# Four raw buffers for w_out, and three Newton steps for the reciprocal root, in a fused attention and two-layer kernel

## The chip, the cores and the metric

The kernel runs on one core of a Trainium2 chip. TensorE (PE) does the matmuls, VectorE (DVE) and ScalarE (ACT) the elementwise work, GpSimd (POOL) some of the elementwise products, and SyncE (SP) issues the transfers. The metric is device time in microseconds (us); lower is better.

## The reference

```python
x = attention(q, k, v)            # 4 batches, 8 heads, 576 positions of 64; laid out as [2304, 512]
# layer 1 (512 -> 2048 -> 512); w_in and w_out come as 64-bit floats
h = x @ w_in
g = np.maximum(h, 0.0) + alpha * np.minimum(h, 0.0)
x = g @ w_out
# layer 2 (512 -> 1536 -> 512)
rms = np.sqrt(np.mean(x * x, axis=-1, keepdims=True) + 1e-06)
xn = x / rms * rms_g
g = xn @ w_gate
silu = g * (1.0 / (1.0 + np.exp(-g)))
return silu * (xn @ w_val) @ w_out2
```

The attention is a sum of two: one over positions averaged by fours, and a local one in which each position sees its three neighbours on either side.

## The kernel before

The 2304 tokens are six blocks of 384, each block two chunks of 192. Every dense product is made of three float16 matmuls (high by high, high by low, low by high), so every operand is split into a high and a low half: ACT writes the high half (L345) and DVE the low one (L346).

The first layer begins in `m1_first`. Its stages `h0`, `h1` and `h2` multiply three chunks by w_in (PE L1250, `hps`); ACT and DVE apply the slope and split the result into `g` tiles (L1254, L1256, L345, L346). A `g` tile holds four of the 16 blocks f of 128 hidden columns, and the tiles stay in memory until `o0` and `o1` multiply them by w_out (PE L1263, `acc`). For chunk 0 the four tiles lie in the weight pool under the tags u12 (f = 0 to 3), u0 (4 to 7), u1 (8 to 11) and u2 (12 to 15).

Before that the weights have to be prepared. They arrive as 64-bit floats and pass through a raw tile `wr`: SP loads half a piece (L999 for w_in, L1009 for w_out), ACT rescales its upper words (L1018), and two DVE instructions put together a 32-bit float (L1020, L1021). Then ACT sums the squares (L1031). w_in comes in six pieces whose decoded floats `wc` lie under u0 to u5, three blocks f in each: u1 holds f = 3, 4, 5 and u2 holds f = 6, 7, 8, until `split_in` has made the float16 halves `wi` of those blocks. w_out comes in pieces 0 to 4 of three blocks and piece 5 of one; half of a large piece is 768 columns of 8 bytes in 128 partitions (768 KB), loaded by two transfers of 512 KB and 256 KB. Its raw tiles have two homes in a pool with one buffer per tag: `xh` for the first halves and `x1` for the second (piece 5 uses `xh` for both). A half can be loaded only when DVE has read the half that was there before. When all 16 blocks are squared, `scale_out` (PE L319 `allps`, then short DVE instructions to L1082) gives the scales, and `split_out` turns each block into `wo` (L345, L346). The floats of block f lie one place behind the halves of block f, so one split has to read before the next can write.

In program order, the 30 preparation steps of w_out are woven into stage `h0`, `scale_out` and nine splits into `h1`, and the rest into `h2`. What runs when is settled by `issue_order`: it lists every instruction with its operands, takes the use of a buffer by two tiles in turn as a dependency, simulates the engines with its own costs, and fixes the order of every engine's queue (SP's too), best of 20 rounds. Each queue then runs strictly in that order. A tile that is given a buffer whose earlier tile still has later readers in program order is placed behind those readers.

The second layer's `rms_tasks` normalise a block: squares, a sum over partitions, then `ssum`, which finds one over the root in tile `ry` from a bit trick (L1200, L1202) and Newton steps of three DVE instructions each (L1205, L1206, L1207) on three columns. A matmul spreads it (L1213) and DVE applies it (L1224). There are six such blocks; the first belongs to stage `o1`.

Of the kernel before, what the change touches and what calls it, by code (L numbers as in the profile page):

```python
# [234 lines left out]
def kernel(  # L235
# [19 lines left out]
    NF = FF // 128  # L255
# [88 lines left out]
    def split(hi, lo, src, s):  # L344
        nc.scalar.activation(out=hi, in_=src, func=AF.Copy, scale=s)  # L345
        nc.vector.scalar_tensor_tensor(out=lo, in0=src, scalar=s, in1=hi, op0=ALU.mult, op1=ALU.subtract)  # L346
# [684 lines left out]
                nc.scalar.activation(out=o, in_=src, func=AF.Square, accum_out=acc[:, i:i + 1])  # L1031

    p1 = [Piece(w_in, f"u{i}", c0=i * UC, n=min(UC, FF - i * UC)) for i in range(6)]
    p1o = [Piece(w_out, None, f0=3 * i, nf=min(3, NF - 3 * i), raw=("xh", "x1" if i < 5 else "xh")) for i in range(6)]
    RING = (3, 4, 6, 7, 5, 12, 0, 1, 2, 8, 9, 10, 11)
    W2_ORDER = [0, 4, 8, 1, 5, 9, 2, 6, 10, 3, 7, 11]
    W2_AT = {i: n for n, i in enumerate(W2_ORDER)}
# [128 lines left out]
    def rms_tasks(m):  # L1166
        st = {}

        ne = KK if m == 0 else 1

        def sq(e):
            def f():
                a = x1_p.tile([128, BW], F32, tag=("ra", "rb")[e % 2 if ne > 1 else e > 0], name="ra")
                nc.scalar.activation(out=a, in_=x1_t[m][:, e], func=AF.Square)
                if ne == 1 and e == 0:
                    st["a"] = a
                    return
                if ne == 1:
                    nc.vector.tensor_tensor(out=st["a"], in0=st["a"], in1=a, op=ALU.add)
                    if e < KK - 1:  # L1180
                        return
                    a = st["a"]
                if "ps" not in st:
                    st["ps"] = ps_t.tile([128, NT, ne], F32, tag="at", name="ssps")
                for t in range(NT):
                    nc.tensor.matmul(st["ps"][:, t, e % ne:e % ne + 1], a[:, t * 128:(t + 1) * 128], ones,
                                     start=True, stop=True)
            return f

        NT = BW // 128  # L1190

        def ssum():
            v_ = x1_p.tile([128, 3, NT], F32, tag="ry", name="ry")
            x, y, t_ = v_[:, 0], v_[:, 1], v_[:, 2]
            p = st["ps"][:, :, 0]
            if ne > 1:
                nc.vector.tensor_reduce(out=x, in_=st["ps"], axis=AX.X, op=ALU.add)
                p = x
            nc.vector.tensor_scalar(out=x, in0=p, scalar1=1.0 / DM, scalar2=1e-6, op0=ALU.mult, op1=ALU.add)
            nc.vector.tensor_scalar(out=y.bitcast(I32), in0=x.bitcast(I32), scalar1=1, scalar2=None,  # L1200
                                    op0=ALU.logical_shift_right)
            nc.vector.tensor_scalar(out=y.bitcast(I32), in0=y.bitcast(I32), scalar1=-1.0, scalar2=float(0x5F3759DF),  # L1202
                                    op0=ALU.mult, op1=ALU.add)
            for _ in range(4):
                nc.vector.tensor_tensor(out=t_, in0=y, in1=y, op=ALU.mult)  # L1205
                nc.vector.scalar_tensor_tensor(out=t_, in0=t_, scalar=-0.5, in1=x, op0=ALU.mult, op1=ALU.mult)  # L1206
                nc.vector.scalar_tensor_tensor(out=y, in0=t_, scalar=1.5, in1=y, op0=ALU.add, op1=ALU.mult)  # L1207
            st["y"] = y

        def bcast():  # L1210
            ps = ps_t.tile([128, BW], F32, tag="at", name="rps")
            for t in range(NT):
                nc.tensor.matmul(ps[:, t * 128:(t + 1) * 128], st["y"][:, t:t + 1].to_broadcast([128, 128]), ident,  # L1213
                                 start=True, stop=True)
            st["r"] = ps

        def xn(e):
            def f():
                if e == 0:
                    p_ = (xt_p, "xt") if m >= NBLK - 2 else (x1_p, "xh")  # L1220
                    st["xh"] = p_[0].tile([128, 2, KK, BW], F16, tag=p_[1], name="xh")
                    xh_t[m] = st["xh"]
                x = x1_t[m][:, e]
                nc.vector.tensor_tensor(out=x, in0=x, in1=st["r"], op=ALU.mult)  # L1224
                split(st["xh"][:, 0, e], st["xh"][:, 1, e], x, 2.0 ** P_N)
            return f

        return [sq(e) for e in range(KK)] + [ssum, bcast] + [xn(e) for e in range(KK)]

    xh_t = {}  # L1230
# [343 lines left out]
```

## Time and profile before

| | |
|---|---|
| time, median of 3 runs | 1074.2 us (1073.49 to 1074.56) |
| the profiled execution | 1076.26 us, of which its span is 1074.6 us |
| PE busy | 990.3 us (92%) |
| DVE busy | 711.3 us (66%) |
| ACT busy | 476.9 us (44%) |
| POOL busy | 144.8 us (13%) |

A busy share is an average over stages. The rows below are times in us from the start of the span. A bracket in a row of an engine's timeline is idle time before the instruction and what ended it. The granted clock (PEclk) is a share of TensorE's full clock.

### The profile page before, as it was taken

To read this page: it belongs to the slowest core of one execution; us is meant where nothing else is said; L and a number is where in the kernel's file an instruction comes from. 1 tells how busy PE (TensorE), PEld (TensorE's weight loads), DVE (VectorE), ACT (ScalarE), POOL (GpSimd) and SP (SyncE) were. 2 spreads that over 40 slices of the span, in tenths; PEclk is the share of its full clock that TensorE was granted. 3 is DMA by queue.
4 is the path that set the end of the run, shared out by engine and by line. 5 is a ranking of instruction groups with operands and counts; after the bars stand their busy time and mean duration, and the time that the engine had idled before them with its cause. 6 is when DMAs were issued, how large, how long until landed. Compare 5 with 4: busy or idle time off the path is not lost.

```text
span 1074.6 us, 16316 instructions
## 1 busy us (share of the span) xinstructions
PE 990.3 (92%) x6232; PEld 617.2 (57%) x6232; DVE 711.3 (66%) x1533; ACT 476.9 (44%) x1178; POOL 144.8 (13%) x118
## 2 busy tenths in 40 slices
PE   2698999769999997989999999999999999999996
PEld 2465567556996554555655555565556655555553
DVE  1557899899988788999854699993344252352321
ACT  2975878324778855443455323341133331221211
POOL 2412221232000123212100232310000000000000
PEclk9999979689999998999999999999999999999998
DMA  9964454301464422312012212100010000100000
GB/s 166 191 145 131 131 166 149 113 30 59 122 185 142 143 88 74 118 45 91 14 50 58 95 34 74 30 1 1 1 30 1 1 1 1 31 1 2 28 1 30
DMA packets 49972, 74.54 MB, mean 69 GB/s; under 512 B 17682, under 2 KB 30886, under 8 KB 49894
## 3 DMA queue, kind: packets, MB, share of 16 engines
q1 hardware_dynamic: 49894, 73.50, 24.4%
q8 instruction: 49, 0.80, 0.3%
q14 instruction: 29, 0.24, 0.1%
HBM read 68.76 MB, written 4.72 MB: 68 GB/s over the span
## 4 chain that ended last, share of the span: by engine, by line
PE 73%; DVE 13%; DMA 7%; ACT 4%; issue 1%; SPq 1%; POOL 1%; ACTq 0%; POOLq 0%; DVEq 0%
PE gps L1342 21%; PE hps L1250 16%; PE acc L1263 15%; PE oacc L1367 10%; DMA out_dram<-ob 4%; DVE prod L508 2%; PE lsps L837 1%; PE avps L649 1%; PE sps L610 1%; DVE prod L495 1%; DMA wr<-in_moe_w_out_dram 1%; DVE wc L1021 1%; PE avps L808 1%; PE lops L891 1%; DVE ls L458 1%
## 5 line engine op out<-in xcount | busy, mean ns | idle before, releaser
L1250 PE MATMUL hps<-xt,wi 128*128 128x192 f16 (+1 forms) x1536 | 335.1, 298 | 8.5 <-DVE g L346 7.7
L1342 PE MATMUL gps<-xh,w 128*128 128x384 f16 x1728 | 338.7, 327 | 0.6 <-DVE uhl L1359 0.6
L1263 PE MATMUL acc<-ghl,wo 128*128 128x384 f16 (+1 forms) x960 | 239.7, 312 | 4.6 <-ACT ghl L345 2.4
L1342 PEld LDWEIGHTS <-w 128*128 128x128 f16 x1728 | 169.8, 99 | 117.6 <-issue 4.1
L1367 PE MATMUL oacc<-w,uhl 128*128 128x512 f16 x648 | 192.4, 379 | 4.0 <-ACT ob L1397 2.6
L1250 PEld LDWEIGHTS <-wi 128*128 128x128 f16 x1536 | 153.5, 103 | 72.8 <-issue 21.2
L1263 PEld LDWEIGHTS <-wo 128*128 128x128 f16 x1344 | 130.6, 100 | 75.1 <-issue 10.8
L1353 DVE SCALAR_TENSOR_TENSOR th<-th,gps 128x384 f32<-128x384 f32 x72 | 39.8, 552 | 146.5 <-ACT th L1351 146.5
L1351 ACT ACTIVATE th<-gps,tsc 128x384 f32<-128x384 f32 x72 | 41.9, 581 | 147.6 <-PE gps L1342 147.4
L1367 PEld LDWEIGHTS <-uhl 128*128 128x128 f16 x648 | 63.9, 99 | 71.8 <-issue 3.7
L1256 DVE SCALAR_TENSOR_TENSOR hps<-g,oma,hps 128x192 f32<-128x192 f32 (+1 forms) x128 | 66.1, 516 | 44.3 <-ACT g L1254 43.6
L1254 ACT ACTIVATE g<-hps 128x384 f32<-128x384 f32 x96 | 47.1, 490 | 106.1 <-PE hps L1250 105.4
L447 POOL TENSOR_TENSOR prod<-cq,ckv 128x896 f32<-128x896 f32 x24 | 54.2, 2259 | 288.4 <-ACT w L345 114.4
L1358 ACT ACTIVATE uhl<-gps 128x384 f16<-128x384 f32 x72 | 35.4, 491 | 108.1 <-DVE gps L1356 102.1
L1263 PE MATMUL acc<-g,wo 128*128 128x384 f16 (+1 forms) x384 | 67.1, 297 | 6.9 <-DVE wo L346 5.1
L495 POOL TENSOR_TENSOR prod<-ls,ckv 128x896 f32<-128x896 f32 x24 | 44.0, 1835 | 139.8 <-DVE lo L508 66.6
L508 DVE TENSOR_TENSOR prod<-prod 128x384 f32<-128x384 f32 (+1 forms) x108 | 58.4, 551 | 4.9 <-POOL prod L495 4.9
L1359 DVE TENSOR_TENSOR uhl<-gps,uhl 128x384 f16<-128x384 f32 x72 | 40.0, 555 | 31.5 <-ACT uhl L1358 31.5
L345 ACT ACTIVATE ghl<-hps,sc 128x384 f16<-128x384 f32 x72 | 41.7, 579 | 38.6 <-DVE hps L1256 37.6
L458 DVE TENSOR_REDUCE ls<-prod 128x14 f32<-128x896 f32 x54 | 57.3, 1075 | 0.0
L346 DVE SCALAR_TENSOR_TENSOR ghl<-hps,sc,ghl 128x384 f16<-128x384 f32 x72 | 43.9, 611 | 14.9 <-ACT ghl L345 14.5
L1020 DVE TENSOR_SCALAR wc<-wr 128x768 int32<-128x768 int32 (+1 forms) x38 | 21.2, 561 | 36.7 <-ACT wr L1018 36.6
(229 smaller groups left out, 1245.3 us busy)
## 6 DMA issues: line engine op xcount, KB each, us to landing
wr<-in_moe_w_out_dram SPq DMA_DIRECT2D x18, 512.0 KB
wr<-in_moe_w_in_dram SPq DMA_DIRECT2D x20, 384.0 KB
wr<-in_moe_w_gate_dram SPq DMA_DIRECT2D x8, 768.0 KB
wr<-in_moe_w_val_dram SPq DMA_DIRECT2D x8, 768.0 KB
ckv<-in_k_dram SPq DMA_DIRECT2D x7, 768.0 KB
ckv<-in_v_dram SPq DMA_DIRECT2D x7, 768.0 KB
wr<-in_moe_w_out_dram SPq DMA_DIRECT2D x20, 256.0 KB
out_dram<-ob SPq DMA_DIRECT2D x13, 256.0 KB
```

What stands on the lines that cost most here:

```text
L346: nc.vector.scalar_tensor_tensor(out=lo, in0=src, scalar=s, in1=hi, op0=ALU.mult, op1=ALU.subtract)
L447: engs[i].tensor_tensor(out=pr, in0=view(st["q"][:, j, t:t + TP], [[D, TP], [0, ND], [1, D]]), in1=view(st["k"][:, j, t:t + TP], [[D, TP], ...
L458: nc.vector.tensor_reduce(out=st["s"][:, j, t:t + TP], in_=st.pop(("p", i)), axis=AX.X, op=ALU.add)
L495: engs[i].tensor_tensor(out=pr, in0=view(st["s"][:, j, t:t + TP], [[ND, TP], [1, ND], [0, D]]), in1=view(st["v"][:, j, t:t + TP], [[D, TP] ...
L508: add = lambda o, a, c: nc.vector.tensor_tensor(out=o, in0=a, in1=c, op=ALU.add)
L1250: nc.tensor.matmul(ps[:, j], wi[:, f + j, a, kk * 128:(kk + 1) * 128], x[:, b_, kk, c0:c0 + n], start=(i == 0), stop=(i == 3 * KK - 1))
L1254: nc.scalar.activation(out=g, in_=ps, func=AF.Relu, scale=-1.0)
L1256: nc.vector.scalar_tensor_tensor(out=ps[:, j], in0=g[:, j], scalar=oma[:, f + j:f + j + 1], in1=ps[:, j], op0=ALU.mult, op1=ALU.add)
L1263: nc.tensor.matmul(acc[e], wo_f(f)[:, a, e * 128:(e + 1) * 128], hl[:, b_], start=(f == 0 and i == 0), stop=(f == NF - 1 and i == 2))
L1342: nc.tensor.matmul(ps, w2_t[i0 + f // 3].rearrange("p a (k c) -> p a k c", k=KK)[:, a, kk, (f % 3) * 128:(f % 3 + 1) * 128], xh[:, b_, kk] ...
L1351: nc.scalar.activation(out=th, in_=gp, func=AF.Tanh, scale=tsc[:, f // 3:f // 3 + 1])
L1367: nc.tensor.matmul(acc[tt], t[:, a, tt * 128:(tt + 1) * 128], w[:, b_, f % 3], start=(f in first and i == 0), stop=(f in last and i == 2))
```

## The change

Pieces 1 and 3 of w_out take their raw tiles from the tags u1 (first half) and u2 (second half); pieces 0, 2, 4 and 5 stay as they were. The loop of Newton steps runs three times.

```diff
-    p1o = [Piece(w_out, None, f0=3 * i, nf=min(3, NF - 3 * i), raw=("xh", "x1" if i < 5 else "xh")) for i in range(6)]
+    p1o = [Piece(w_out, None, f0=3 * i, nf=min(3, NF - 3 * i), raw=(("xh", "x1"), ("u1", "u2"))[i % 2] if i < 5 else ("xh", "xh")) for i in range(6)]
...
-            for _ in range(4):
+            for _ in range(3):
                 nc.vector.tensor_tensor(out=t_, in0=y, in1=y, op=ALU.mult)
                 nc.vector.scalar_tensor_tensor(out=t_, in0=t_, scalar=-0.5, in1=x, op0=ALU.mult, op1=ALU.mult)
                 nc.vector.scalar_tensor_tensor(out=y, in0=t_, scalar=1.5, in1=y, op0=ALU.add, op1=ALU.mult)
```

## Rows read from the trace of the kernel before

**Rows 1.** Stretches: busy time (instructions) of PE, PEld, DVE, ACT, POOL; PEclk; DMA share; GB/s.

```profile
100.00:130.00 30.00, 24.52 (x134) 15.54 (x134) 21.69 (x57) 23.65 (x87) 7.46 (x3) 1.00 0.48 137
130.00:190.00 60.00, 53.75 (x424) 39.68 (x423) 56.51 (x122) 46.51 (x133) 11.84 (x9) 0.89 0.48 153
190.00:210.00 20.00, 13.54 (x82) 11.12 (x82) 16.88 (x33) 6.25 (x13) 4.49 (x3) 0.61 0.36 118
210.00:270.00 60.00, 50.08 (x385) 35.49 (x384) 58.74 (x107) 21.54 (x37) 17.75 (x9) 0.90 0.16 54
300.00:400.00 100.00, 100.00 (x778) 69.37 (x776) 83.77 (x198) 75.03 (x196) 8.36 (x3) 1.00 0.43 139
500.00:1040.00 540.00, 534.14 (x3159) 309.19 (x3158) 296.85 (x611) 168.24 (x371) 41.73 (x23) 1.00 0.08 25
```

**Rows 2.** SP's timeline: issues of w_out's loads (start, duration, line, count).

```profile
105.65 0.38 SPq L1009 DMA_DIRECT2D wr<-in_moe_w_out_dram  x1
...
131.21 2.57 SPq L1009 DMA_DIRECT2D wr<-in_moe_w_out_dram  x4
142.38 4.71 SPq L1009 DMA_DIRECT2D wr<-in_moe_w_out_dram  x4
154.74 2.68 SPq L1009 DMA_DIRECT2D wr<-in_moe_w_out_dram  x4
165.01 0.82 SPq L1009 DMA_DIRECT2D wr<-in_moe_w_out_dram  x2
...
190.66 0.34 SPq L1009 DMA_DIRECT2D wr<-in_moe_w_out_dram  x1
```

**Rows 3.** SP's waits, 90 to 200 us: in total, times, longest.

```profile
SPq L1009 <- DVE wo L1021: 26.2, 8, 6.2
```

**Rows 4.** PE's timeline, 200 to 240 us.

```profile
201.84 0.61 PE L319 MATMUL allps<-s,ones 128*128 128x16 f32 x2 [2.78 <-ACT sqs L1031]
...
207.78 5.83 PE L1263 MATMUL acc<-g,wo 128*128 128x384 f16 x24 [1.31 <-ACT wo L345]
...
238.01 1.46 PE L1263 MATMUL acc<-g,wo 128*128 128x384 f16 x4 [3.79 <-DVE wo L346]
```

**Rows 5.** Waits of all engines, 100 to 300 us: in total, times, longest.

```profile
ACT wo L345 <- DVE wo L346: 18.6, 11, 4.1
PE acc L1263 <- DVE wo L346: 5.1, 3, 3.8
PE acc L1263 <- ACT wo L345: 1.9, 2, 1.3
```

**Rows 6.** The chain that ended last: a run of `acc` matmuls later on.

```profile
707.82 1.46 PE acc L1263 x9
```

**Rows 7.** DVE's timeline: splits of w_in and of `g`, decoding of w_out.

```profile
86.56 0.75 DVE L346 SCALAR_TENSOR_TENSOR wi<-wc,swi,wi 128x512 f16<-128x512 f32 x1
126.64 0.74 DVE L346 SCALAR_TENSOR_TENSOR wi<-wc,swi,wi 128x512 f16<-128x512 f32 x1
159.78 0.61 DVE L346 SCALAR_TENSOR_TENSOR g<-hps,sc,g 128x384 f16<-128x384 f32 x1
163.99 0.95 DVE L1021 SCALAR_TENSOR_TENSOR wo<-wr,wo 128x768 int32<-128x768 int32 x1
169.20 0.95 DVE L1021 SCALAR_TENSOR_TENSOR wo<-wr,wo 128x768 int32<-128x768 int32 x1
170.07 0.61 DVE L346 SCALAR_TENSOR_TENSOR g<-hps,sc,g 128x384 f16<-128x384 f32 x1
```

**Rows 8.** Tile `ry`: count, duration in ns (min/median/max), first and last start.

```profile
L1205 DVE TENSOR_TENSOR ry<-ry x24: 100/160/165, 283.8 to 943.4; 128x3 f32<-128x3 f32 x24
L1206 DVE SCALAR_TENSOR_TENSOR ry<-ry x24: 153/159/165, 284.0 to 943.5; 128x3 f32<-128x3 f32 x24
L1207 DVE SCALAR_TENSOR_TENSOR ry<-ry x24: 152/164/1329, 284.5 to 943.7; 128x3 f32<-128x3 f32 x24
```

## The prediction

> **What bounds the kernel now.** I read the page's engine totals and its 40 slices first: PE is busy 92% of the span, and nearly all that is missing lies before 500 us. So I cut the span into stretches [rows 1]. From 500 to 1040 us PE is busy 534.14 of 540 us and from 300 to 400 us all of 100: there PE alone sets the end, and no saving on DVE, ACT or a queue is worth anything. Between 100 and 270 us it is another picture. From 210 to 270 us DVE is busy 58.74 of 60 us and PE only 50.08; from 130 to 190 us DVE 56.51 and PE 53.75; and from 190 to 210 us PE is busy 13.54 of 20 us at a mean granted clock of 0.61, that is, for part of the time at the lower of its levels, 1.2 GHz. In that short stretch DVE too has 3.12 us free. So somebody else is late there.
>
> Third came the queue of transfers and its waits. The loads of w_out leave SP in groups [rows 2]: 131.21 for piece 1, 142.38 for piece 2, 154.74 for piece 3, 165.01 for the first half of piece 4, 190.66 for the last half piece. That is a step of (165.01 - 131.21) / 3 = 11.3 us per piece. SP waits 26.2 us in eight waits at those loads for the last DVE instruction of decoding [rows 3], which is what empties a raw buffer. So the pieces do not overlap: a load, a decode, the next load into the same buffer.
>
> Fourth came PE's own timeline at the end of that chain [rows 4]. PE stands 2.78 us before the sum of squares that opens `scale_out`, 1.31 us before the first matmul with w_out, and 3.79 us in the middle of that stage for a split of w_out. The list of waits adds them up [rows 5]: 5.1 us on DVE's half of the split and 1.9 us on ACT's. The splits are a chain of their own, because each must read a place before the next writes it: ACT waits 18.6 us for DVE there.
>
> **The change part by part.** *Raw buffers.* No work of an engine is removed: the same 22 loads, 12 rescalings and 24 DVE instructions of decoding. What changes is who waits. Now `xh` holds pieces 0 to 5 in turn; its seven fillings (piece 5 fills it twice) become five. Two steps of 11.3 us go, so the chain of loads could end up to 22.6 us earlier if nothing else held it. From below it is nothing, if DVE has no room to decode earlier. DVE has some: it is idle 8.31 us from 100 to 130 us, 3.49 from 130 to 190 and 3.12 from 190 to 210 [rows 1], and decoding one half costs it about 1.5 us.
>
> What would an earlier end be worth? The time that PE loses directly to w_out being late is 2.78 us at the sum of squares, and 5.1 + 1.9 = 7.0 us at the splits [rows 4, 5]: 9.8 us. Behind the first of these PE also ran slowly: the 24 matmuls from 207.78 us took 5.83 us, 0.243 each, and nine of the same line later on take 1.46, 0.162 each [rows 4, 6], so 24 x 0.081 = 1.9 us more. That makes 11.7 us at the most. It is not all to be had, because from 210 to 270 us DVE is full (1.26 us idle), and a split of w_out that comes earlier pushes a product of the local attention, which waits in the same queue, to a later place. There is room for such work from 300 to 400 us, where DVE is idle 16.23 us beside a full PE. Between 0 and 11.7 I take half of the direct waits, 4.9 us, because the first wait and the early part of the splits lie where DVE has room, and the later ones where it has none.
>
> *What the new buffers wait for.* u1 is free when DVE has split f = 5 of w_in, the sixth of its splits, at 87.3 us; u2 when it has split f = 8, the ninth, at 127.4 us [rows 7]. So the first half of piece 1 can be fetched long before 131.21 us, and the second only 3.8 us before. A load that waits in SP's queue holds what stands behind it, here the windows of v for the next chunks. Today SP waits there 26.2 us in all, so I count no new loss. Four issues move, at 0.38 us or less each [rows 2], and 768 KB more are on the way early, 0.79 MB at the 153 GB/s of the stretch, some 5 us. The transfers cover it: their engines are 48% busy from 100 to 130 us [rows 1]. Without that cover those 5 us would go to the loads of v.
>
> *What waits for the new buffers.* u1 and u2 are also the homes of `g` for f = 8 to 15 of chunk 0. ACT's split of f = 8 must now wait until DVE has decoded the first half of piece 3, and f = 12 until the second half. Behind it on ACT stand all rescalings and splits, and two PSUM banks further PE stops. Today the low half of f = 8 begins at 159.78 us and piece 3 is decoded to 164.94; f = 12 begins at 170.07 and its half is decoded at 170.15 [rows 7]. If piece 3 came no sooner the price is 164.94 - 159.78 = 5.2 us; if it comes two steps sooner, nothing. I take nothing, since piece 1 no longer queues behind piece 0.
>
> *Newton steps.* One step less in six blocks is 18 DVE instructions, at medians 160, 159 and 164 ns [rows 8], 0.48 us a block and 2.9 us in all. The first block runs at 283.8 us, the others from 501 us on, where PE is full [rows 1] and block after block is prepared one stage ahead. So five of them are worth nothing; PE's matmuls hide them, and if that cover were gone they would cost 0.48 us each. The first lies close behind the stretch in which DVE is the limit; between 0 and 0.48 us I take 0.3.
>
> The sum: 4.9 + 0.3 = 5.2 us less. On the profiled execution that is 1076.26 - 5.2 = 1071.1 us. The median of the runs is 2.06 us below that execution, so the forecast there is 1069.0 us.
>
> **The rivals.** *DVE is the limit, and nothing comes of it.* From 130 to 190 and from 210 to 270 us DVE is busy 115.25 of 120 us [rows 1], and the change takes no instruction from it there. A w_out that is ready earlier only trades places with other work of DVE. For it: the splits that made PE wait 3.79 us lie where DVE is full. Against it: the waits from 190 to 210 us, where DVE is not. Then only the 0.48 us of the first block is left, and the time is 1073.7 us. The Trainium skill says so as a rule (Perfetto Trace Analysis, "Identifying the Most-Contended Engine"): improve the engine with the highest occupancy first. The trace agrees that this is DVE from 210 to 270 us, at 58.74 of 60 us; by that rule alone the buffers give nothing, and the sum would be 1073.7 us.
>
> *Everything is given back.* If the splits start a step or two earlier and DVE's other work goes to 300 to 400 us, PE gets all 11.7 us and the 0.48 us: 1062.0 us. For it: PE's idle time from 190 to 270 us is 16.4 us, so there is that much to fill. Against it: DVE has only 1.26 us free from 210 us on.
>
> *Slower: the shared homes.* The `g` of f = 8 waits for piece 3, at the price of 5.2 us worked out above: 1079.4 us. For it: today the two are that far apart in the wrong order, and ACT's queue is strict. Against it: piece 1 starts early. It decides from the point where piece 3's first half is decoded later than the split of f = 8 would begin. The order of every queue is also found anew; that moves places, but it has no price of its own that the trace shows.
>
> **How the numbers follow.** The forecast (1069.0 us; 1066 to 1072 by itself) gets 0.35, the full return (1062.0) 0.20, nothing (1073.7) 0.25 and the shared homes (1079.4) 0.20. A measurement of this kernel tells about 0.2%, 2.1 us, from no change: above 1076.3 us is slower, below 1072.1 faster. So faster 0.55, same 0.25, slower 0.20. The range runs from 1060, a little beyond the full return, to 1079, which leaves out about half of the slower case and less than 0.1 below.
>
> **What would show it.** In the profile of the changed kernel the last load of w_out should be issued before 180 us instead of 190.66, the sum of squares should open `scale_out` before 190 us instead of 201.84, and PE's waits for `wo` should be under 5 us instead of 7.0. PE should then reach its full stretch before 265 us, and the stages from 500 us on should be as long as now. If DVE is the limit, the loads are earlier and the first `acc` matmul is not. If the shared homes cost, ACT's split of `g` waits for L1021 around f = 8, with PE idle behind it. The prediction is wrong if the loads of w_out keep their step of 11 us, or if the time from 300 us to the end changes by more than 2 us.

## The result, and the profile after

The changed kernel takes 1060.88 us (median of 4 runs, 1059.96 to 1063.09) where the kernel before took 1074.38, measured with it (4 runs, 1073.49 to 1075.95): a ratio of 0.9869 [0.984, 0.9899], 13.5 us less. The forecast was 5.2 us less. The profiled execution took 1061.15 us, its span 1059.4; the span of before was 1074.6, so the two traces differ by 15.2 us.

The stretches of after, read as [rows 1]; the sixth row is one that the prediction had not read for before:

```profile
100.00:130.00 30.00, 23.04 (x125) 14.18 (x126) 26.21 (x62) 23.56 (x89) 4.33 (x2) 1.00 0.53 163
130.00:190.00 60.00, 52.34 (x411) 40.59 (x410) 55.11 (x119) 43.72 (x126) 14.84 (x10) 0.83 0.45 140
190.00:210.00 20.00, 14.78 (x123) 12.11 (x124) 19.80 (x40) 7.43 (x14) 5.64 (x3) 0.91 0.30 99
210.00:270.00 60.00, 46.80 (x357) 33.36 (x355) 58.70 (x111) 24.38 (x48) 13.92 (x7) 0.94 0.23 74
300.00:400.00 100.00, 98.79 (x754) 67.48 (x752) 85.39 (x203) 74.84 (x194) 11.18 (x6) 1.00 0.39 121
400.00:500.00 100.00, 97.25 (x569) 56.00 (x569) 96.49 (x208) 43.25 (x88) 21.39 (x11) 1.00 0.25 82
500.00:1040.00 540.00, 537.00 (x3175) 310.59 (x3174) 287.89 (x578) 167.94 (x369) 40.26 (x22) 1.00 0.08 23
```

And the same sixth stretch of the kernel before:

```profile
400.00:500.00 100.00, 90.55 (x504) 50.84 (x502) 92.97 (x195) 45.30 (x91) 24.64 (x12) 0.95 0.23 75
```

Between 100 and 270 us, where the prediction looked for the gain, little has changed: PE is busy 136.96 of 170 us against 141.89, at a mixed clock. DVE has filled the holes of the first and third stretch (26.21 and 19.80 us against 21.69 and 16.88). The large difference is from 400 to 500 us: PE 97.25 us busy against 90.55, and 569 matmuls begun against 504.

The loads of w_out on SP's timeline, for [rows 2]:

```profile
93.14 0.36 SPq L1009 DMA_DIRECT2D wr<-in_moe_w_out_dram  x1
...
104.77 0.45 SPq L1009 DMA_DIRECT2D wr<-in_moe_w_out_dram  x1
...
136.96 1.30 SPq L1009 DMA_DIRECT2D wr<-in_moe_w_out_dram  x3
...
160.02 0.82 SPq L1009 DMA_DIRECT2D wr<-in_moe_w_out_dram  x2
171.03 0.35 SPq L1009 DMA_DIRECT2D wr<-in_moe_w_out_dram  x1
182.11 0.35 SPq L1009 DMA_DIRECT2D wr<-in_moe_w_out_dram  x1
```

The loads begin 12.5 us earlier and follow each other more closely at first, but the last two steps, 160.02 to 171.03 and 171.03 to 182.11, are still 11 us each, and the last load is only 8.55 us earlier (182.11 against 190.66). PE's timeline, for [rows 4], shows what became of that:

```profile
191.59 0.39 PE L319 MATMUL allps<-s,ones 128*128 128x16 f32 x2 [2.15 <-ACT sqs L1031]
...
201.47 1.80 PE L1263 MATMUL acc<-g,wo 128*128 128x384 f16 x10 [0.46 <-ACT wo L345]
...
227.85 2.29 PE L1263 MATMUL acc<-g,wo 128*128 128x384 f16 x12 [1.39 <-DVE wo L346]
236.19 2.94 PE L1263 MATMUL acc<-g,wo 128*128 128x384 f16 x16 [1.34 <-DVE wo L346]
253.51 1.46 PE L1263 MATMUL acc<-g,wo 128*128 128x384 f16 x4 [3.27 <-DVE wo L346]
```

The sum of squares is 10.25 us earlier, the first `acc` matmul 6.3, and at 253.51 PE still waits 3.27 us for a split. The list of waits from 100 to 300 us, for [rows 5], with the waits for `g` as well:

```profile
PE hps L1250 <- DVE g L346: 12.2, 9, 3.0
ACT wo L345 <- DVE wo L346: 9.3, 8, 2.0
PE acc L1263 <- DVE wo L346: 6.0, 3, 3.3
PE allps L319 <- ACT sqs L1031: 2.1, 1, 2.1
PE acc L1263 <- ACT wo L345: 0.7, 2, 0.5
```

PE's waits for `wo` are 6.7 us, against 7.0; its waits for `g` are 12.2 us, where the same view of before has 7.7:

```profile
PE hps L1250 <- DVE g L346: 7.7, 4, 3.5
```

To see where the time came from, the span is cut at three instructions of ACT that every version has: the first evacuation of block 0 of the first layer (L1277), that of block 2, and the first output `ob` (L1397). First after, then before:

```profile
269.92 1.37 ACT L1277 ACTIVATE x<-acc,inv 128x192 f32<-128x192 f32 x4 [0.59 <-PE acc L1263]
...
408.68 1.07 ACT L1277 ACTIVATE x<-acc,inv 128x192 f32<-128x192 f32 x3
...
631.96 0.69 ACT L1397 ACTIVATE ob<-oacc,sc 128x512 f32<-128x512 f32 x1 [1.30 <-PE oacc L1367]
```

```profile
270.80 1.05 ACT L1277 ACTIVATE x<-acc,inv 128x192 f32<-128x192 f32 x3 [1.46 <-PE acc L1263]
...
414.13 0.42 ACT L1277 ACTIVATE x<-acc,inv 128x192 f32<-128x192 f32 x1 [2.48 <-PE acc L1263]
...
645.66 0.69 ACT L1397 ACTIVATE ob<-oacc,sc 128x512 f32<-128x512 f32 x1 [2.52 <-PE oacc L1367]
```

So the part with w_out in it gave 0.9 us (270.80 to 269.92), the part to block 2 another 4.6 (143.33 to 138.76), the part to the first output 8.2 (231.53 to 223.28), and all the rest 1.5 (428.9 to 427.4). 12.8 of 15.2 us came after w_out had been prepared, where the change edits nothing but one Newton step. The parts hold the same matmuls but for 5 to 7 each, about 1 us by the 0.162 us of [rows 6] (an estimate). One wait there has a name: PE for the sums of squares of the second layer's weights. Before, from PE's timeline:

```profile
408.93 0.38 PE L319 MATMUL allps<-s,ones 128*128 128x3 f32 x2 [2.10 <-ACT sqs L1031]
...
463.69 0.38 PE L319 MATMUL allps<-s,ones 128*128 128x3 f32 x2 [3.13 <-ACT sqs L1031]
```

After, the only such wait from 340 to 566 us:

```profile
398.68 0.38 PE L319 MATMUL allps<-s,ones 128*128 128x3 f32 x2 [0.54 <-ACT sqs L1031]
```

5.2 us have become 0.54, and behind them the granted clock no longer falls: 1.00 from 400 to 500 us against 0.95. A mean of 0.95 over 100 us is some 10 us at the lower level, 1.2 GHz, which costs at most 5 us (an estimate). Over the whole run PE does its 6232 matmuls in 977.4 us against 990.3, at a mean granted clock of 0.982 against 0.973, and its idle time (span less busy) is 82.0 against 84.3 us. These sums hide where the gain lies. Up to the first cut PE was 7.5 us less busy and 6.6 us more idle, which all but cancels. Behind it, before and then after:

```profile
270.80:1074.60 803.80, 777.47 (x4896) 469.54 (x4894) 507.53 (x1092) 317.13 (x722) 74.72 (x38) 0.99 0.16 50
```

```profile
269.92:1059.40 789.48, 772.10 (x4889) 467.51 (x4887) 497.89 (x1059) 311.33 (x709) 72.83 (x38) 1.00 0.16 48
```

Of 14.3 us there, 9.0 are less idle time of PE (17.4 us against 26.3) and 5.4 a shorter busy time. Why would a buffer for w_out do that?

### The profile page after: what moved, and what is told of

It is laid out like the page before. It is cut to its first block, busy times and chain, and to the rows that moved or that the text cites. A ratio compares the mean times of both kernels' runs of the same rounds, so it can differ in the third digit from the quotient of the medians.

```text
span 1059.4 us, 16284 instructions
## 1 busy us (share of the span) xinstructions
PE 977.4 (92%) x6232; PEld 612.9 (58%) x6232; DVE 710.2 (67%) x1515; ACT 473.7 (45%) x1178; POOL 143.4 (14%) x118
## 4 chain that ended last, share of the span: by engine, by line
PE 68%; DVE 17%; ACT 5%; DMA 5%; issue 2%; SPq 1%; POOL 1%; ACTq 0%; DVEq 0%; POOLq 0%
PE gps L1342 22%; PE hps L1250 14%; PE acc L1263 13%; PE oacc L1367 11%; DMA out_dram<-ob 3%; DVE prod L508 2%; PE avps L649 2%; DVE hps L1256 2%; DVE prod L495 2%; PE lsps L837 2%; DMA sdv<-in_v_dram 1%; DVE lo L508 1%; DVE wc L1021 1%; PE sps L610 1%; DVE wo L346 1%
## 5 line engine op out<-in xcount | busy, mean ns | idle before, releaser
L1250 PE MATMUL hps<-xt,wi 128*128 128x192 f16 (+1 forms) x1536 | 335.8, 299 | 14.9 <-DVE g L346 12.2
L1263 PE MATMUL acc<-ghl,wo 128*128 128x384 f16 (+1 forms) x960 | 237.0, 310 | 0.6 <-ACT ob L1397 0.6
L1359 DVE TENSOR_TENSOR uhl<-gps,uhl 128x384 f16<-128x384 f32 x72 | 39.9, 555 | 31.5 <-ACT uhl L1358 31.3
L508 DVE TENSOR_TENSOR prod<-prod 128x384 f32<-128x384 f32 (+1 forms) x108 | 53.4, 509 | 7.8 <-POOL prod L495 7.8
L458 DVE TENSOR_REDUCE ls<-prod 128x14 f32<-128x896 f32 x54 | 57.3, 1075 | 0.0
L1356 DVE SCALAR_TENSOR_TENSOR gps<-th,kap,gps 128x384 f32<-128x384 f32 x60 | 37.3, 621 | 13.5 <-PE gps L1342 9.1
```

Source lines behind the costliest of these rows:

```text
L458: nc.vector.tensor_reduce(out=st["s"][:, j, t:t + TP], in_=st.pop(("p", i)), axis=AX.X, op=ALU.add)
L508: add = lambda o, a, c: nc.vector.tensor_tensor(out=o, in0=a, in1=c, op=ALU.add)
L1250: nc.tensor.matmul(ps[:, j], wi[:, f + j, a, kk * 128:(kk + 1) * 128], x[:, b_, kk, c0:c0 + n], start=(i == 0), stop=(i == 3 * KK - 1))
L1263: nc.tensor.matmul(acc[e], wo_f(f)[:, a, e * 128:(e + 1) * 128], hl[:, b_], start=(f == 0 and i == 0), stop=(f == NF - 1 and i == 2))
```

## The experiments

Theory A: the four buffers let DVE work ahead; by 200 us it has been busy 143.7 us against 134.3 before, 9.4 us more, and that lead fills the later stages. Its rivals: theory B, that the lead is nothing and the particular order that `issue_order` found for this kernel is what counts; theory C, that it is the shorter Newton loop. The kernels ran in three groups of four (e1 to e4, e5 to e8, e9 to e12), each in 5 rounds beside the kernel before on one chip, another chip for each group; medians in us, with the lowest and highest run.

**Each edit alone.** `e1_buffers_only` has the line of raw tiles and four steps, `e2_newton_only` `range(3)` and the old line.

> Raw buffers of pieces 1 and 3 in u1 and u2, four Newton steps kept. Theory A (the buffers let DVE decode w_out in its early idle time, and DVE carries that lead to the stretch from 340 to 650 us): nearly all of the 13.5 us, so 1060 to 1064 us. Theory B (the gain is an accident of finding the order of every queue anew): anywhere from 1062 to 1080 us. Theory C (the Newton step made it): 1074 us.

> Three Newton steps, two raw buffers. Theory A: within 1 us of before, 1073.5 us. Theory B: the order is found anew here too, so it may lie as much as 10 us from 1074 us on either side. Theory C: 1061 us.

Measured: buffers alone 1072.5 (1064.77 to 1076.39, 12 runs) against 1075.54, 0.9958 [0.9931, 0.9984]; Newton alone 1075.28 (1065.87 to 1080.84, 12 runs), 0.9992 [0.9963, 1.0021]. Together that is 3.3 us, not 13.5, and even the favourable ends of both intervals (7.4 and 4.0 us) stay below it: the edits don't add up.

**The homes at one order.** Both kernels are planned with the dependencies of both sets of homes, so that every queue has the same order in both; only the buffers differ. In `e3_common_order_old_homes` the raw tiles of pieces 1 and 3 count as users of u1 and u2 but stay in `xh` and `x1`; in `e4_common_order_new_homes` the other way round. Both take four Newton steps.

```diff
-        ring.setdefault(t.tag, []).append(t.name)
+        [ring.setdefault(g, []).append(t.name) for g in [t.tag] + [x.tag for x in tc.info.tiles if x.tag.startswith(ALSO.get(t.name, "?") + "_")][:1]]
...
-            before[n] = old
+            before.setdefault(n, set()).update(old)
...
+                ALSO.update({r.tensor.name: ("u1", "u2")[half]} if w is w_out and self.f0 in (3, 9) else {})
```

> Two raw buffers and four Newton steps, but the order of the queues is found with the dependencies of both kinds of homes at once (xh and x1 as well as u1 and u2 for pieces 1 and 3), so that the same order can be run with either. Theory A: such an order can use none of the new freedom, 1074 to 1079 us. Theory B: within 10 us of 1074 us on either side.

> Exactly the order of e3 in every queue, but pieces 1 and 3 go through u1 and u2. If the waits for the raw buffers are themselves the cost, 5 us or more below e3. If the gain comes only from an order that uses the new freedom (theory A, and theory B in another way), within 2 us of e3.

Measured: old homes 1071.05 (1069.49 to 1078.04, 12 runs), 0.9966 [0.9945, 0.9986]; new homes 1071.58 (1069.13 to 1073.62, 12 runs), 0.9961 [0.9943, 0.9979]. At this order the buffers are worth nothing, 0.5 us the wrong way. Theory A had asked for 1074 to 1079 us here. The order is neither that of before nor that of after, and was planned under the waits of both; that the new homes could be worth something at an order of their own is not excluded by this pair.

**Other orders of the same kernels.** One number in the planner is moved by less than 1.5%; what is computed is untouched, and the queues come out in another order.

```diff
-        return 2300 if eng[a] == "SP" else waits.get((eng[a], eng[b]), 100)
+        return 2310 if eng[a] == "SP" else waits.get((eng[a], eng[b]), 100)
```

in `e5_before_other_order_1` and `e6_changed_other_order_1`, and

```diff
-            return 69 + n / (1.92 if fast else 0.96) + 60 * (extra > 0)
+            return 70 + n / (1.92 if fast else 0.96) + 60 * (extra > 0)
```

in `e7_before_other_order_2` and `e8_changed_other_order_2`.

> The kernel before, with one number of the order's own costs changed (the lag behind a transfer 2310 instead of 2300): same work and buffers, another order in every queue. Theory A (the buffers cause the gain): 1073 to 1077 us. Theory B (the order found decides, whatever the edit): away from 1075 us by 3 us or more, on either side.

> The changed kernel with the same one number changed. Theory A: 1060 to 1064 us again, 10 us or more below e5. Theory B: no nearer to 1061 than to 1075 us.

> The kernel before with another number of the order's costs changed (the fixed part of a DVE instruction 70 instead of 69). Theory A: 1073 to 1077 us. Theory B: away from 1075 us by 3 us or more.

> The changed kernel with that number changed. Theory A: 1060 to 1064 us, 10 us or more below e7. Theory B: no nearer to 1061 than to 1075 us; the mean of the three changed orders would lie less than 5 us below that of the three orders of before.

Measured, against 1075.75 for the kernel before in those rounds:

| order | kernel before | changed kernel |
|---|---|---|
| as planned | 1075.75 | 1060.88 (measured apart, 4 runs) |
| 1 | 1073.45 (1071.27 to 1076.68), 0.9977 [0.996, 0.9994] | 1068.75 (1065.19 to 1077.76), 0.9948 [0.9918, 0.9978] |
| 2 | 1067.47 (1063.52 to 1069.79), 0.9916 [0.9886, 0.9946] | 1077.53 (1069.66 to 1082.95), 1.0006 [0.9976, 1.0036] |

An order of before is 8 us faster than before, an order of the changed kernel no faster than before. The orders spread by 8 us for the one and 17 us for the other; the means of three differ by 3 us (1072.2 and 1069.1). The 17 us rest on 1060.88, from another group of runs; side by side the changed kernel's orders 1 and 2 differ by 9 us. e6, e7 and e8 lie outside what theory A had asked for; e5 lies inside it (1073 to 1077) and not as far from 1075 us as theory B had. Like after and before, the two versions with order 2 differ in the stretch from 400 to 500 us: here before, then the changed kernel.

```profile
400.00:500.00 100.00, 92.28 (x529) 52.32 (x528) 97.76 (x198) 43.03 (x89) 23.16 (x11) 0.98 0.24 80
```

```profile
400.00:500.00 100.00, 89.63 (x498) 49.95 (x497) 91.86 (x186) 44.93 (x91) 24.39 (x12) 0.95 0.22 73
```

That stretch alone does not rank the versions: in e5 PE is busy only 88.14 us there, in an execution 6 us shorter than that of e8. Nor is the wait for the sums of squares the mark of a slow order: from 340 to 566 us it is 1.7 us in e7 and 1.9 in e8. In e8 PE waits instead for DVE's splits `uhl` of the second layer (L1359), which the same view of e7 does not have:

```profile
PE gps L1342 <- DVE uhl L1359: 3.1, 2, 2.0
PE oacc L1367 <- DVE uhl L1359: 2.5, 1, 2.5
```

**The order of after, with the fourth step.** In `e9_changed_order_fourth_step` the 18 DVE instructions of a fourth Newton step stand in the changed kernel's order of every queue, planned at no cost (`free_`); all else keeps its place.

```diff
-    dur = [cost(k, *aps[k]) for k in count]
+    ...; dur = [0.0 if k in free_ else cost(k, *aps[k]) for k in count]
...
-        return 2300 if eng[a] == "SP" else waits.get((eng[a], eng[b]), 100)
+        return 0 if b in free_ else 2300 if eng[a] == "SP" else waits.get((eng[a], eng[b]), 100)
...
-            for _ in range(3):
+            for _ in range(4):
```

> The changed kernel in its own order of every queue, but with the fourth Newton step put back behind the third in all six blocks (18 more DVE instructions, which the order counted at nothing). If the step is hidden, as the prediction had it: 1060.5 to 1062.5 us, the time of the changed kernel. If the Newton step were the gain: 1064 us or more.

Measured: 1067.67 (1064.93 to 1069.95, 6 runs) against 1074.69, 0.9931 [0.9914, 0.9947]. That is on the Newton side of what was recorded, as if 18 short instructions cost 6.8 us. The trace puts most of it elsewhere. ACT's timeline at the three cuts, and the added line's tile:

```profile
276.85 1.37 ACT L1277 ACTIVATE x<-acc,inv 128x192 f32<-128x192 f32 x4 [0.72 <-PE acc L1263]
...
415.60 1.07 ACT L1277 ACTIVATE x<-acc,inv 128x192 f32<-128x192 f32 x3
...
639.46 0.69 ACT L1397 ACTIVATE ob<-oacc,sc 128x512 f32<-128x512 f32 x1 [1.30 <-PE oacc L1367]
```

```profile
L1205 DVE TENSOR_TENSOR ry<-ry x24: 143/164/165, 291.0 to 936.5; 128x3 f32<-128x3 f32 x24
```

It is 6.9 us late at 276.85 us, before the first Newton step at 291.0. From there its parts are those of after: 138.75, 223.86 and 428.0 us against 138.76, 223.28 and 427.4. So 1.2 us of the 8.1 between the two spans lie where the added instructions can act, and 6.9 where both kernels have the same queues. In the stretch from 120 to 140 us PE ran at its lower level the whole time in this execution (0.50), while after had 0.75 there; in both, PE had been partly idle in the 20 us before (14.70 and 13.51 us busy). First e9, then after:

```profile
100.00:120.00 20.00, 14.70 (x77) 8.94 (x78) 17.77 (x45) 16.76 (x66) 2.82 (x2) 1.00 0.52 153
120.00:140.00 20.00, 20.00 (x90) 11.80 (x90) 16.51 (x35) 10.68 (x31) 3.98 (x2) 0.50 0.51 162
```

```profile
100.00:120.00 20.00, 13.51 (x66) 8.35 (x67) 17.80 (x44) 16.77 (x70) 2.08 (x1) 1.00 0.43 130
120.00:140.00 20.00, 18.98 (x111) 12.60 (x109) 17.64 (x42) 12.92 (x37) 5.80 (x3) 0.75 0.63 194
```

Only one execution of each has a trace, and the changed kernel was not run again beside it, so how often it would lose those microseconds itself stays open. A low clock in one execution does not account for all of it: every run of e9 lies above every run of after (1064.93 against 1063.09), and the two at a mean clock of 0.981 and 0.987, about that of after or above it, took 1064.93 and 1065.33. So the only repetition of that order, with a fourth step, was 7.0 us faster than the kernel before, not 13.5.

**DVE's lead at the order of before.** Two kernels keep the order of before and take work off DVE. In `e10_before_order_thin_w_out` L1021 goes over every 32nd column of w_out only (`::z`, planned at its old cost), in `e11_before_order_thin_layer2` over those of 24 halves of the second layer's weights. They leave out the low bits of the weights in the other 31 of 32 columns.

```diff
-            nc.vector.scalar_tensor_tensor(out=d, in0=lo, scalar=29, in1=d,
+            nc.vector.scalar_tensor_tensor(out=d[:, :, ::z], in0=lo[:, :, ::z], scalar=29, in1=d[:, :, ::z],
```

> The kernel before in its own order of every queue, but the last decoding instruction of w_out (L1021) works on every 32nd column only, so that the low bits of w_out are left out: 9.5 us less of DVE between 130 and 201 us. If DVE's full stretch sets the time: 5 to 9.5 us less, 1066 to 1071 us. If it does not (theory B, the order and TensorE's clock decide): within 2.5 us of 1075.5.

> The same for the weights of the second layer (24 halves, low bits left out): some 21 us less of DVE between 186 and 462 us, order as before. If DVE sets the time up to 500 us: 10 us or more below before, 1065 us or less. If not: within 2.5 us of 1075.5.

Measured against 1074.69: thin w_out 1072.28 (1067.22 to 1074.32, 12 runs), 0.9966 [0.9947, 0.9985]; thin layer 2 1067.94 (1065.62 to 1076.58, 9 runs), 0.994 [0.9916, 0.9965]. By the medians of L1021's rows (950 ns to 191 for the ten wide halves of w_out, 951 to 210 for the 24 of the second layer) 7.6 and 17.8 us were taken away; 2.4 and 6.7 came back, about a third (by the intervals 1.6 to 5.9 and 3.8 to 9.0 us). Both times lie between what was recorded for the two theories and meet neither. PE still stands at the same sums of squares as in the kernel before. Its waits from 340 to 566 us in the trace with thin w_out:

```profile
PE allps L319 <- ACT sqs L1031: 5.2, 2, 3.1
```

That is the 5.2 us of before, to the tenth, and with thin layer 2 it is 4.6. So a lead of DVE does not remove this wait; another order does.

**A shorter chain still.** `e12_changed_last_half_in_ob` gives the second half of piece 5 a home of its own in the changed kernel; the order is found anew.

```diff
-... if i < 5 else ("xh", "xh")) for i in range(6)]
+... if i < 5 else ("xh", "ob")) for i in range(6)]
```

> The changed kernel, and the second half of piece 5 goes through the idle tile tag ob instead of xh, so that the last link of the chain of loads falls away; order found anew. If a shorter chain of w_out is what gains (theory A): at or below the changed kernel, 1054 to 1061 us. If the order found decides (theory B): anywhere from 1060 to 1078 us.

Measured: 1073.55 (1069.37 to 1077.49, 12 runs) against 1074.69, 0.9992 [0.9973, 1.0012]. One buffer more, in an order found anew, and the gain is gone. PE's waits for the sums of squares from 340 to 566 us are 7.1 us in this trace.

The parts of the span between the three cuts, from ACT's timeline of each profiled execution:

| kernel | to block 0 | to block 2 | to first output | to the end |
|---|---|---|---|---|
| before | 270.8 | 143.3 | 231.5 | 428.9 |
| after | 269.9 | 138.8 | 223.3 | 427.4 |
| e9, order of after, four steps | 276.9 | 138.8 | 223.9 | 428.0 |
| e1, buffers alone | 279.1 | 142.0 | 223.8 | 427.6 |
| e2, Newton alone | 281.3 | 143.0 | 225.3 | 429.5 |
| e3 / e4, common order | 266.7 / 267.4 | 147.3 / 147.6 | 230.1 / 228.7 | 426.5 / 426.3 |
| e5, before, order 1 | 264.5 | 145.0 | 233.0 | 427.2 |
| e6, changed, order 1 | 273.8 | 144.2 | 228.5 | 429.7 |
| e7, before, order 2 | 275.0 | 140.3 | 224.3 | 426.8 |
| e8, changed, order 2 | 272.4 | 144.0 | 232.1 | 427.3 |
| e10 / e11, order of before | 263.6 / 266.5 | 143.1 / 142.4 | 232.7 / 228.8 | 428.6 / 428.5 |
| e12, one more home | 269.4 | 145.5 | 230.7 | 427.9 |

The two kernels with the order of after agree to 0.6 us in each of the last three columns, and so do the two of the common order in all but one (1.4 us). The third column splits the versions into 223 to 225 and 228 to 233 us, and kernels of either set of homes and of either number of steps stand in both. The first column is the stage with w_out: without the thin kernels, the five versions with the old homes reach its end at 271.7 us in the mean and the seven with the new ones at 272.7. Each row is one execution (of e2 and e6 the slowest), and with the same queues after and e9 differ by 6.9 us there. None of these beats the changed kernel; the nearest are e7, e9 and e11 with 1067.5 to 1067.9.

## Why the prediction came out as it did

The time fell, as forecast, and lies within the range, near the low end. The mechanism was not the one that the sum paid for, and as far as the sum goes the hit is luck: of the 9.8 us of direct waits that it priced, 8.85 are still there (2.15 at the sum of squares, 6.7 for `wo`).

- **Raw buffers, the chain of loads.** Half right. The first load is issued at 93.14 us and PE is busy without a gap from 255 to 300 us, sooner than the 265 us that were forecast. But the last two steps are still 11 us, the last load was to leave before 180 us and left at 182.11, and the sum of squares was to come before 190 us and came at 191.59. Of the possible 22.6 us of chain, 8.55 were had.
- **Raw buffers, 4.9 us.** Wrong in place. PE's waits for `wo` were to fall below 5 us and stayed at 6.7; the wait at the sum of squares went from 2.78 to 2.15 us; the waits for `g` rose by 4.5. To the first evacuation the two traces differ by 0.9 us, less than the 6.9 us between two executions of the same queues (after and e9), and at a common order the homes are worth nothing (e3 and e4). The reason given for "nothing", that DVE is full from 210 to 270 us (58.70 of 60 in after too), held in that stretch.
- **Shared homes.** Taken as nothing, and no run shows a price: in the trace of after no split of `g` on ACT waits for L1021, after and e9 have the homes and the best later parts, and e4 stands 0.5 us from e3.
- **Newton steps, 0.3 us.** Not contradicted. e2 measures no change within 0.4% either way; at the order of after everything behind the first evacuation differs by 1.2 us between three steps and four, in one pair of executions. That bounds it from above and cannot tell 0.3 from it.
- **The order.** This is the step that failed: "The order of every queue is also found anew; that moves places, but it has no price of its own that the trace shows." The trace of one order cannot show it; three orders of one kernel do, with 8 and 17 us between them. That is more than the whole forecast. The same two edits took 1068.75 and 1077.53 us in two other orders, so the 13.5 us belong to this one order more than to the edits.
- **What was left out of the stretches.** The prediction read 300 to 400 and 500 to 1040 us, found PE full, and did not read 400 to 500, where PE was busy 90.55 us at a clock of 0.95. Its own test, "if the time from 300 us to the end changes by more than 2 us", is what the cuts met: 4.6 + 8.2 + 1.5 us from block 0 on. The Trainium skill (Perfetto Trace Analysis, "Optimization Strategy") has the reader look, regime by regime, for the gaps of the engine that limits and for what each gap waits for. The trace bears that out: in this stretch it leads to the two waits for sums of squares, 5.2 us, of which after has 0.54 left.
- **The rival "Everything is given back".** Its time, 1062.0 us, is 1.1 us from the result, by coincidence: it expected 11.7 us from PE's waits between 190 and 270 us, and most of these are still there.

By the Trainium skill (Perfetto Trace Analysis, "Identifying the Most-Contended Engine") the engine with the highest occupancy comes first, which the prediction read as DVE before 270 us. e10 and e11 show how far that carries at a fixed order: by the medians about a third of the time taken off DVE comes back.

What is shown is that an order alone moves the kernel before by 8 us and the changed kernel by 9 to 17 (e5 to e8), that at the order of after the fourth step costs at most 1.2 us from block 0 on in one pair of traces (e9), and that at one common order the homes are worth nothing (e3 and e4). That the order, and not the homes, makes the 13.5 us is argued from these: the order of after was never run with the old homes, and none of the orders of before that were tried reached it (1067.47 at best). What stays open is whether that order needs the new homes, why it places the sums of squares and the splits of the second layer so well, and how much of the 13.5 us a repetition would keep; e9, the nearest to one, kept 7.0.

## What to carry to other kernels

Where a program finds the order of all queues anew, run the unchanged kernel under two or three trivially different orders first: an edit is known only beyond their spread, here 8 to 17 us. To price an edit itself, hold the order: plan both versions with the dependencies of both, or plan an added instruction at no cost and a shrunken one at its old cost. And cut the two traces at instructions that both have before believing any account of a gain: here 12.8 of 15.2 us lay behind the stage that was edited.

## What the runs showed of the hardware

One and the same program varied by up to 15 us, in most cases in step with the granted clock: the kernel before, beside e9 to e12, took 1068.8 us in a run at a mean clock of 0.980 and 1083.4 at 0.966, buffers alone 1064.8 at 0.984 and 1076.4 at 0.969. The clock is not all of it: the 12 runs of e4, at 0.977 to 0.985, lie within 4.5 us and do not follow it. So the 2.1 us that the prediction took as told from no change, from three runs within 1.1 us, were too little. In the traces the lower level is granted between 120 and 280 us and, in all but after and e9, again between 404 and 471, in or just behind stretches in which PE had been partly idle: in the kernel before, PE was busy 15.51 us from 400 to 420 at a mean of 0.83. e9 lost 6.9 us in the first of these stretches with the same queues as after. A few runs made together, as the four of after at 0.980 to 0.982, do not show this spread.
